# RWKV-5 attention and squared-ReLU MLP on one core: a new loading head, v through GpSimd's queue, and a new order table

## The chip, the core and the metric

The kernel runs on one core of a Trainium2 chip. Time is device time in microseconds; of the kernel before there are three runs, with a median of 171.05 us (170.32 to 171.6). The profile shown is of one execution.

## The reference

Four sequences (B), eight heads (H), 768 tokens (S) and 48 numbers a head (D). For every batch and head a 48x48 state is carried over the tokens, and the 8x48 = 384 outputs of a token go through a two-layer MLP with 2048 hidden numbers:

```python
for t in range(S):
    kt, vt, rt = k[:, :, t], v[:, :, t], r[:, :, t]
    cur = np.einsum('bhd,bhe->bhde', u[None] * kt, vt)
    y[:, :, t] = np.einsum('bhd,bhde->bhe', rt, state + cur)
    state = w[None, :, :, None] * state + np.einsum('bhd,bhe->bhde', kt, vt)
x = y.transpose(0, 2, 1, 3).reshape(B * S, H * D)
h = x @ w_in
return np.maximum(h, 0.0) ** 2 @ w_out
```

Inputs and output are float32; the kernel multiplies in bfloat16 and adds in float32.

## The kernel before

The tokens are cut into six chunks of 128. A chunk of one sequence is a *unit*; unit i is chunk i // 4 of sequence i % 4, so there are 24. A unit's attention goes through these steps, each a function and a word of the order table:

- `rt`, `kt`, `vt`: its r, k and v are loaded, 192 KB each, 128 tokens on the partitions. `scale` (VectorE) multiplies r and k by powers of w that depend on the token, into `rkw`.
- r and k are turned so that head numbers lie on the partitions (`rkT`). For units 0 to 5, the head of the program, TensorE does it (`turn`, x = 0 for r and 1 for k) and ScalarE copies it out (`rkT`). From unit 6 on two units go together: one DMA transpose on SyncE's queue (`rkD`).
- `at` is the product of k and r for each head, `mask` (VectorE) keeps its upper triangle, `y` multiplies it by v and adds the state's share; `dv` and `yb` (VectorE) add the token's own term and write y in bfloat16. `d` or `s` give that term's sums, and `s` also the unit's own state, which `sadd`, `sdec` and `stb` add up for the next chunk.
- `y` is turned into `xT`, by TensorE for units 0 to 5 (`xturn`, `xT`) and by a DMA transpose for pairs (`xD`).

The MLP of a unit follows: `m1` is a quarter (a pair's eighth) of the first layer, `relu` (ScalarE) and `sqA` or `sqD` (square on ScalarE or VectorE) make g, `m2` is a quarter of the second layer, `osb` copies its sum out and `out` stores it. From unit 6 on `m1` works on two units at once. The weights come by GpSimd's queue with a cast, in quarters `I` and `O`.

In the head, r and k of units 0 to 5 are loaded so that a partition holds four tokens in a row of one pair of heads; a load is then two transfers of 96 KB, one for the even heads and one for the odd, with runs of four tokens (768 bytes) in memory. k in that layout isn't in token order, which the state needs, so that after the first turn k is turned back (`kb`, four TensorE transposes, and `kbT`, a ScalarE copy). v of units 0 to 5 comes by GpSimd's queue in token order, 192 KB a transfer; r, k and v of the later units come by SyncE's queue in pairs of 384 KB, in token order, whose runs in memory are one token of one head (192 bytes).

What stands where is written out by hand: the program goes through the words of `ORDER`, `name.unit.part@bank`, and each issues its instructions. Every engine and every queue runs its own instructions in that order and waits for semaphores; nothing reorders them. `fill.n` is n products of a constant tile on TensorE with no use of the result. PSUM has eight banks, which the number behind `@` names; a bank is used again when its reader is done.

Of the kernel before, what the change touches and what calls it, by code (L numbers as in the profile page):

```python
# [16 lines left out]
kt.0.0 kt.0.1 rt.0.0 rt.1.0 I.0 rt.1.1 vt.0 ktA.1.0 lnat.0 fill.26 log@4567 kt.1.1 lnat.1 ids rt.2.0 w.1 upper w.0  # L17
fill.8 cols@1 rt.2.1 wk scale.0.0 kt.2.0 zeros scale.0.1 wr fill.8 turn.0.0@2 kt.2.1 copied uwb turn.0.1@5 rkT.0.0
rt.3.0 rkT.0.1 vt.1 rk.0 fill.10 at.0@63 scale.1.0 rt.3.1 I.3 kb.0@4 mask.0.0 d.0@2 turn.1.0@7 I.2 kbT.0 kt.3.0
mask.0.1 rkT.1.0 vt.2 scale.1.1 vb.0 I.1 kt.3.1 fill.19 turn.1.1@4 dv.0 y.0@3 rkT.1.1 rt.4.0 yb.0 vb.1 rk.1 fill.9  # L20
kb.1@4 kt.4.0 scale.2.0 at.1@31 xturn.0@6 rt.4.1 mask.1.1 d.1@5 turn.2.0@2 xT.0 rkT.2.0 scale.2.1 kt.4.1 fill.5
m1.0.0@7 kbT.1 mask.1.0 turn.2.1@2 relu.0.0 dv.1 rt.5.0 fill.2 y.1@1 rkT.2.1 m1.0.3@4 yb.1 end rt.5.1 s.1@5
scale.3.0 relu.0.3 wend xturn.1@7 rk.2 at.2@26 xT.1 kb.2@0 mask.2.1 sqA.0.0 kt.5.0 d.2@4 turn.3.0@3 vt.3 s.0@7
sadd.1 rkT.3.0 m1.0.2@1 kt.5.1 scale.3.1 kbT.2 O.0 m1.1.0@6 mask.2.0 vb.2 relu.0.2 vt.4 turn.3.1@3 dv.2 m1.1.3@5
rt.6 rkT.3.1 sadd.0 O.1 y.2@1 relu.1.0 kt.6 m1.1.2@0 yb.2 relu.1.3 vt.5 at.3@72 rk.3 relu.1.2 kb.3@4 mask.3.1
xturn.2@6 sqA.1.0 O.2 m1.0.1@5 scale.4.0 xT.2 s.2@0 O.3 sqD.0.3 d.3@2 relu.0.1 m1.1.1@1 vb.3 mask.3.0 turn.4.0@3
kbT.3 m1.2.0@6 scale.4.1 relu.1.1 dv.3 m1.2.1@4 rkT.4.0 sqD.1.3 sqA.0.2 y.3@7 m1.2.2@1 scale.5.0 relu.2.1 sqD.1.1
m1.2.3@2 relu.2.2 sqD.0.1 s.3@5 sqA.1.2 turn.4.1@4 m2.0.0@3 sadd.3 relu.2.3 sadd.2 m2.1.0@1 rkT.4.1 yb.3 relu.2.0
m2.1.1 rk.4 vb.4 scale.5.1 kb.4@7 stb.1 xturn.3@6 at.4@42 kbT.4 m2.0.1 mask.4.1 xT.3 stb.0 s.4@5 mask.4.0 turn.5.0@6
m1.3.0@2 sqD.2.1 rkT.5.0 y.4@0 dv.4 relu.3.0 turn.5.1@6 rt.8 sadd.4 m1.3.3@7 rkT.5.1 yb.4 m2.1.2 sqA.3.0 sqA.2.0  # L30
m2.0.2 kt.8 xturn.4@2 m2.0.3 xT.4 scale.6.0 kb.5@5 osb.0 m2.1.3 scale.7.0 relu.3.3 m1.3.1@2 vtS.6 kbT.5 vb.5
m1.4.0@6 scale.6.1 scale.7.1 at.5@75 relu.4.0 m2.2.0@0 mask.5.0 osb.1 rkD.6 sqA.4.0 m1.4.1@4 sqD.2.3 sqA.2.2 sqD.3.3
m1.4.2@1 relu.3.1 mask.5.1 m2.2.1 stb.3 sdec.4 m1.4.3@6 relu.4.2 rt.10 rk.5 y.5@5 sqA.4.2 scale.8.0 s.5@2 scale.8.1
relu.4.1 m2.2.2 scale.9.0 relu.4.3 vtS.8 m1.3.2@1 sqD.3.1 stb.4 m2.3.0@4 dv.5 relu.3.2 yb.5 m2.2.3 scale.9.1 kt.10
m2.3.1 osb.2 sadd.5 sqA.4.1 m2.4.0@1 sqD.4.3 vb.6 xturn.5@0 sdec.5 at.6@2376 xT.5 rk.6 rkD.8 m2.4.1 stb.2 mask.7.0
stb.5 m1.5.0@0 sqA.3.2 mask.6.0 s.7@7 relu.5.0 mask.7.1 m1.5.3@5 mask.6.1 s.6@2 relu.5.3 m2.4.2 dv.6 out.0 vb.8
y.6@3 dv.7 rt.12 y.7@0 yb.6 m1.5.1@6 yb.7 m2.3.2 sadd.6 relu.5.1 xD.6 scale.10.0 m2.4.3 sqA.5.0 scale.10.1 sqA.5.1
m2.3.3 sadd.7 vtS.10 osb.4 m1.5.2@6 scale.11.1 scale.11.0 m2.5.0@3 relu.5.2 sqD.5.3 kt.12 m2.5.1 sqA.5.2 rk.8
at.8@1520 osb.3 sdec.6 m2.5.2 mask.9.0 rkD.10 m2.5.3 mask.8.0 s.8@4 mask.8.1 osb.5 s.9@2 m1.6.0@7 mask.9.1 m1.6.1@6
sadd.8 relu.6.0 dv.9 kt.14 m1.6.3@5 relu.6.1 dv.8 m1.6.7@1 sqA.6.0 scale.12.0 sadd.9 sqA.6.1 y.9@3 rt.14 y.8@4 vb.10  # L40
m1.6.2@0 yb.8 stb.6 m1.6.5@2 yb.9 relu.6.3 sdec.9 xD.8 m1.6.4@6 relu.6.5 scale.12.1 m2.7.0@3 relu.6.2 sqD.6.3
relu.6.7 vtS.12 m2.6.0@4 scale.13.0 relu.6.4 scale.13.1 m1.6.6@7 sqA.6.2 rk.10 at.10@6120 sqA.6.4 rkD.12 m2.6.1
relu.6.6 mask.10.0 sqA.6.5 s.10@5 sdec.7 m2.7.1 sqA.6.6 sqD.6.7 m2.7.2 stb.7 mask.10.1 stb.9 out.1 m2.7.3 sadd.10
kt.16 mask.11.0 y.10@6 osb.7 m1.8.0@1 dv.10 m1.8.1@2 rt.16 scale.14.0 relu.8.0 sdec.8 m1.8.3@5 relu.8.1 mask.11.1
m2.6.2 stb.8 yb.10 sqA.8.1 s.11@3 y.11@2 relu.8.3 dv.11 m1.8.6@1 vb.12 yb.11 m1.8.4@6 relu.8.6 sadd.11 xD.10 m2.6.3
rk.12 sqA.8.0 relu.8.4 scale.15.0 m1.8.2@2 scale.14.1 m1.8.5@0 relu.8.2 sdec.10 out.4 m2.9.0@7 osb.6 scale.15.1
vtS.14 sqA.8.2 sqD.8.3 m2.8.0@6 relu.8.5 out.3 at.12@4312 sqA.8.6 rkD.14 s.12@0 sqA.8.5 mask.13.0 m2.8.1 sqA.8.4
mask.12.1 m1.8.7@5 mask.12.0 m1.10.1@1 relu.8.7 mask.13.1 out.2 m1.10.3@3 relu.10.1 scale.16.0 vtS.16 s.13@4 sadd.12
y.12@2 dv.12 rt.18 m2.8.2 sdec.11 m1.10.6@5 yb.12 m1.10.5@0 dv.13 relu.10.6 sqD.8.7 y.13@2 stb.10 m2.9.1 relu.10.5
scale.17.0 yb.13 sqA.10.6 m2.8.3 sadd.13 relu.10.3 xD.12 m1.10.2@0 osb.8 sqD.10.3 sqA.10.1 m1.10.0@3 scale.16.1  # L50
kt.18 m1.10.7@1 relu.10.0 scale.17.1 rt.20 at.14@5642 relu.10.2 rk.14 sqA.10.0 m2.9.2 mask.15.1 vb.14 m2.9.3
mask.14.0 rkD.16 relu.10.7 m1.10.4@2 mask.14.1 sqA.10.2 mask.15.0 s.15@5 stb.11 s.14@0 sqA.10.5 m2.11.0@3 dv.14
osb.9 y.14@4 relu.10.4 y.15@6 kt.20 yb.14 vb.16 m2.11.1 sdec.12 sqA.10.4 m2.10.0@1 sadd.15 stb.12 out.5 dv.15
m1.12.0@2 sqD.10.7 m1.12.1@7 relu.12.0 yb.15 m1.12.3@4 scale.18.0 xD.14 scale.18.1 m2.10.1 relu.12.3 scale.19.0
m1.12.7@6 relu.12.1 rt.22 m2.10.2 relu.12.7 out.7 m1.12.2@7 sqA.12.0 vtS.18 sqD.12.7 m2.11.2 sdec.13 relu.12.2
# [28 lines left out]
def kernel(  # L84
# [21 lines left out]
    NH = 6  # L106
# [516 lines left out]
```

## Time and profile before

| | |
|---|---|
| runs | 171.6, 170.32, 171.05 us; median 171.05 |
| profiled execution, first to last instruction (its span) | 170.2 us |
| TensorE busy | 163.9 us, 96% of the span |
| TensorE's weight loads | 134.1 us, 79% |
| ScalarE busy | 129.8 us, 76% |
| VectorE busy | 122.3 us, 72% |
| GpSimd busy | 15.7 us, 9% |
| mean granted TensorE clock | 0.988 |
| read from and written to HBM | 20.50 and 4.72 MB |

The span is what the profile measures between the first and the last instruction; a run's time has a little around it (the median is 0.85 us above this span). Busy time of TensorE counts matmuls whose ends are modelled, so that it says where TensorE had something in its queue rather than what it was worth. The chain of waits lists, in order of time, the pieces of work that the end depended on: start, length, engine and line. In the timeline a row gives start, length, engine, line, operation, output and inputs, and how often, with the idle time before it and what ended it in brackets; `SPq` and `POOLq` are the queues of SyncE and GpSimd, where the length is that of issuing.

### The profile page before, as it was taken

What the parts mean: (1) busy time and instruction counts of PE and PEld (TensorE: products, weight loads), DVE (VectorE), ACT (ScalarE), POOL (GpSimd) and SP (SyncE); (2) the same over time, 40 slices, a digit from 0 to 9 for tenths busy, and PEclk for the clock granted to TensorE, in tenths of its full rate; (3) what the DMA queues carried; (4) which work ended last, traced back from release to release, by engine and by line L of the source; (5) the groups of instructions that cost most, each with busy time, mean ns of one, the idle gap of its engine ahead of it and who ended that gap; (6) DMA issues with size and microseconds to landing.
All of it is one profiled execution on the core that took longest, in us unless ns stands there. A gap on an engine that the chain in (4) does not pass through costs nothing.

```text
span 170.2 us, 4733 instructions
## 1 busy us (share of the span) xinstructions
PE 163.9 (96%) x1947; PEld 134.1 (79%) x1947; DVE 122.3 (72%) x243; ACT 129.8 (76%) x255; POOL 15.7 (9%) x36
## 2 busy tenths in 40 slices
PE   7959999999999999999999999999999999999993
PEld 7649999778787697886977887787889789688672
DVE  6567999876999989988988888989697662101100
ACT  3735999888796489698499679688699739599921
POOL 7770670000000000000000000000000000000000
PEclk9996999999999999999999999999999999999999
DMA  3999999999999899999999997998990501100044
GB/s 92 172 279 240 272 194 254 213 201 227 185 181 218 153 214 190 181 212 191 236 182 202 174 251 173 188 288 197 180 232 4 179 6 54 42 0 4 0 164 162
DMA packets 91493, 28.86 MB, mean 170 GB/s; under 512 B 82864, under 2 KB 90672, under 8 KB 91472
## 3 DMA queue, kind: packets, MB, share of 16 engines
q1 hardware_dynamic: 88416, 23.99, 67.5%
q0 software_dynamic: 2624, 4.33, 12.9%
q8 instruction: 15, 0.25, 0.6%
q10 hardware_dynamic: 432, 0.25, 0.6%
q14 instruction: 6, 0.05, 0.1%
HBM read 20.50 MB, written 4.72 MB: 148 GB/s over the span
## 4 chain that ended last, share of the span: by engine, by line
PE 87%; DMA 6%; DVE 3%; SPq 2%; issue 1%; DVEq 0%
PE bank L493 36%; PE bank L517 34%; DMA rt<-in_r_dram 4%; PE bank L369 4%; PE bank L441 3%; DMA xT<-yb 2%; PE bank L398 2%; PE bank L447 2%; SPq L281 2%; PE bank L533 2%; PE bank L333 1%; PE bank L410 1%; PE bank L345 1%; PE bank L216 1%; PE bank L477 1%
## 5 line engine op out<-in xcount | busy, mean ns | idle before, releaser
L493 PE MATMUL bank<-xT,w_in_q 128*128 128x256 bf16 (+1 forms) x720 | 72.6, 251 | 0.1
L501 ACT ACTIVATE gr<-bank 128x512 f32<-128x512 f32 x96 | 55.3, 604 | 19.0 <-PE bank L493 15.2
L517 PE MATMUL bank<-w_out_q,g 128*128 128x384 bf16 x368 | 68.6, 326 | 0.0
L493 PEld LDWEIGHTS <-w_in_q 128*128 128x128 bf16 x720 | 63.8, 113 | 3.9 <-DMA xT<-yb 0.3
L517 PEld LDWEIGHTS <-g 128*128 128x128 bf16 x368 | 34.3, 98 | 18.1 <-issue 0.2
L508 ACT ACTIVATE g<-gr 128x512 bf16<-128x512 f32 x68 | 41.2, 636 | 0.2
L377 DVE TENSOR_TENSOR am<-bank,smask 128x512 bf16<-128x512 f32 x48 | 31.3, 684 | 7.4 <-PE bank L369 6.6
L510 DVE TENSOR_TENSOR g<-gr 128x512 bf16<-128x512 f32 x28 | 19.0, 686 | 17.2 <-ACT gr L501 17.2
L524 ACT COPY osb<-bank 128x384 f32<-128x384 f32 x23 | 11.0, 480 | 5.7 <-PE bank L517 5.6
L456 DVE TENSOR_TENSOR yb<-bank,dv 128x384 bf16<-128x384 f32 x24 | 12.9, 553 | 3.2 <-PE bank L447 2.3
L420 DVE TENSOR_TENSOR dv<-vb,bank 128x384 f32<-128x384 bf16 x24 | 13.0, 548 | 2.2 <-PE bank L410 1.4
L432 ACT CAST stb<-st 128x384 bf16<-128x384 f32 x20 | 10.2, 522 | 0.6 <-DVE st L428 0.6
L301 DVE TENSOR_TENSOR rkw<-rt,wpos 128x384 bf16<-128x384 f32 x18 | 9.8, 551 | 0.8 <-DMA rt<-in_r_dram 0.7
L301 DVE TENSOR_TENSOR rkw<-kt,wneg 128x384 bf16<-128x384 f32 x18 | 9.7, 551 | 0.8 <-DMA kt<-in_k_dram 0.8
L337 ACT COPY rkT<-bank 128x512 bf16<-128x512 bf16 x12 | 7.0, 590 | 3.4 <-PE bank L333 3.4
L216 PE MATMUL bank<-warm 128*128 128x128 bf16 x87 | 8.4, 265 | 1.1 <-DVE warm L161 1.1
L441 PE MATMUL bank<-vb,am 128*128 128x48 bf16 x192 | 8.9, 185 | 0.0
L428 DVE TENSOR_TENSOR st<-st,wend 128x384 f32<-128x384 f32 x16 | 8.8, 550 | 0.0
L424 DVE TENSOR_TENSOR st<-bank,st 128x384 f32<-128x384 f32 x16 | 8.7, 549 | 0.0
L441 PEld LDWEIGHTS <-am 128*128 128x128 bf16 x192 | 7.9, 97 | 0.8
L369 PE MATMUL bank<-rkT 64*128 64x128 bf16 x192 | 8.2, 221 | 0.2 <-ACT rkT L337 0.2
L216 PEld LDWEIGHTS <-warm 128*128 128x128 bf16 x87 | 7.0, 121 | 1.2 <-DVE warm L161 1.0
(75 smaller groups left out, 120.8 us busy)
## 6 DMA issues: line engine op xcount, KB each, us to landing
out_dram<-osb SPq DMA_DIRECT2D x23, 192.0 KB, 2.4
rt<-in_r_dram SPq DMA_DIRECT2D x9, 384.0 KB, 5.8
kt<-in_k_dram SPq DMA_DIRECT2D x9, 384.0 KB, 5.2
vt<-in_v_dram SPq DMA_DIRECT2D x9, 384.0 KB, 4.5
w_in_q<-in_moe_w_in_dram POOLq DMA_DIRECT2D x4, 384.0 KB, 8.3
w_out_q<-in_moe_w_out_dram POOLq DMA_DIRECT2D x4, 384.0 KB, 8.8
vt<-in_v_dram POOLq DMA_DIRECT2D x6, 192.0 KB, 7.3
kt<-in_k_dram SPq DMA_DIRECT2D x11, 96.0 KB, 5.2
```

Of the source, the lines that this page charges most:

```text
L216: nc.tensor.matmul(out=banks[0][:, :128], lhsT=warm, rhs=warm, start=True, stop=True)
L301: nc.vector.tensor_tensor(t["rkw"][:, x, :, :, :D], pair(src), pair(wneg if x else wpos), ALU.mult)
L369: nc.tensor.matmul(out=t["at"][o][:, p, :], lhsT=t["rkT"][sl, 1, p, :], rhs=t["rkT"][sl, 0, p, :], start=True, stop=True,)
L377: nc.vector.tensor_tensor(am, t["at"][o], smask.unsqueeze(1).to_broadcast([C, HP, C]), ALU.mult)
L420: nc.vector.tensor_tensor(t["dv"], t["vb"], t["d"].unsqueeze(2).to_broadcast([C, H, D]), ALU.mult)
L441: nc.tensor.matmul(out=y[:, 2 * p + o, :], lhsT=t[f"am{o}"][:, p, :], rhs=t["vb"][:, 2 * p + o, :], start=(o == 0 and p == 0), stop=c == 0 ...
L456: nc.vector.tensor_tensor(t["yb"], t["y"], t["dv"].rearrange("p h d -> p (h d)"), ALU.add)
L493: nc.tensor.matmul(out=t["h", s][:, a], lhsT=turned, rhs=chunks[c]["xT"][:, b : b + m, n, :], start=(n == 0), stop=(n == NK - 1),)
L501: nc.scalar.activation(t["gr", s], t["h", s], AF.Relu)
L508: nc.scalar.activation(g, x, AF.Square)
L510: nc.vector.tensor_tensor(g, x, x, ALU.mult)
L517: nc.tensor.matmul(out=t["o"], lhsT=chunks[units[i][0]]["g"][:, f, units[i][1], :], rhs=w_out_q[f // 4][:, f % 4, :], start=(f == 0), stop ...
```

## The change

1. **Head.** r of units 0 to 5 and k of units 0 and 1 keep the layout of four tokens a partition, but come as one transfer of 192 KB. k of units 2 to 5 is loaded in token order by GpSimd's queue, scaled with the token powers `wneg` that the later units use, and turned once; `kb` and `kbT` are left for units 0 and 1 alone. The first transfers are k of unit 0 on ScalarE's queue and r of units 0 and 1 on SyncE's.
2. **Constants.** The identity matrices and the triangle come from one iota on GpSimd and three VectorE comparisons, not from GpSimd's helpers; the ones and zeros under the columns of w and u are set by VectorE.
3. **v.** v of units 6 to 23 comes by GpSimd's queue, one transfer of 192 KB a unit, not by SyncE's in pairs.
4. **Order.** The whole table is new. `fill` products go from 87 to 42, with 34 of them at the very beginning; squares on ScalarE from 68 to 64 and on VectorE from 28 to 32; banks and the order of quarters of `m1` and `m2` differ (`m2` may begin with any quarter).

```diff
 ORDER = """
-kt.0.0 kt.0.1 rt.0.0 rt.1.0 I.0 rt.1.1 vt.0 ktA.1.0 lnat.0 fill.26 log@4567 kt.1.1 lnat.1 ids rt.2.0 w.1 upper w.0
...
+ktA.0 tab rt.1 wu.0 wu.1 upper ids vt.0 I.0 vt.1 lnw lnat.0 fill.33@1 fill.1@0 w.0 log@4567 lnat.1 scale.0.0 w.1
...
-    first = two("rt", 0, loads, [C, H, D], F32)[:, 0]
-    halves = lambda src: src.rearrange("(a o) (q l) d -> o q a (l d)", o=2, l=4)
-    nc.scalar.dma_start(out=first[:, 4:].rearrange("p l d -> p (l d)"), in_=halves(r[0, :, :C])[1])
+    of_two("rt", 0, loads, [C, H, D], F32)
+    by_four = lambda src: src.rearrange("(a o) (q l) d -> q a o (l d)", o=2, l=4)
+    nc.sync.dma_start(out=tiles[0]["rt"].rearrange("p (o l) d -> p o (l d)", o=2), in_=by_four(r[0, :, :C]))
...
+    apart_i = const.tile([128, 128], I32)
+    nc.gpsimd.iota(apart_i, pattern=[[1, 128]], base=0, channel_multiplier=-1)
...
     def identities():
-        make_identity(nc, ident4)
-        make_identity(nc, identb)
+        nc.vector.tensor_scalar(identb, apart_i, 0.0, None, ALU.is_equal)
+        nc.vector.tensor_scalar(ident4, apart_i[:HP, :HP], 0.0, None, ALU.is_equal)
 
     def upper():
-        make_upper_triangular(nc, smask, val=1.0, diag=False)
+        nc.vector.tensor_scalar(smask, apart_i, 0.0, None, ALU.is_gt)
...
+    def turned(i):
+        return i < NH and f" kb.{i}@" in ORDER.replace("\n", " ")
...
+        if i >= NH and not alone:
+            nc.sync.dma_start(out=whole.rearrange("s b h d -> s (b h) d"), in_=both(src, i))
+        elif i < NH and (name == "rt" or turned(i)):
             (queue or nc.sync).dma_start(
-                out=tiles[i][name][:, o * 4 : o * 4 + 4].rearrange("p l d -> p (l d)"), in_=halves(src)[o]
+                out=tiles[i][name].rearrange("p (o l) d -> p o (l d)", o=2), in_=by_four(src[b, :, c * C : (c + 1) * C, :])
             )
+        else:
+            nc.gpsimd.dma_start(out=tiles[i][name], in_=src[b, :, c * C : (c + 1) * C, :].rearrange("h s d -> s h d"))
...
-        if i >= NH:
+        if i >= NH or x and not turned(i):
             nc.vector.tensor_tensor(t["rkw"][:, x, :, :, :D], pair(src), pair(wneg if x else wpos), ALU.mult)
...
-    def load_v(i):
+    def load_v(i, whole_pair=False):
         c, b = units[i]
         whole = of_two("vt", i, loads, [C, H, D], F32)
-        if i >= NH:
+        if whole_pair:
             nc.sync.dma_start(out=whole.rearrange("s b h d -> s (b h) d"), in_=both(v, i))
         else:
             nc.gpsimd.dma_start(out=tiles[i]["vt"], in_=v[b, :, c * C : (c + 1) * C, :].rearrange("h s d -> s h d"))
```

Three places show what the new table does.

**VectorE in the head** (`rkw0` belongs to units 0 and 1, `rkw1` to units 2 and 3; `rt_88` and `kt_155` or `kt_153` are r and k of units 0 and 1, `am` the masked product, `rk` the product r times k). Before:

```order
L303 TENSOR_TENSOR rkw0_127<-rt_88,wfour_123 128x8x48
L303 TENSOR_TENSOR rkw0_127<-kt_155,wfour_123 128x8x48
L253 COPY cols_126<-bank1_77 128x8
L360 TENSOR_TENSOR rk_267<-rkT_241 128x512
L303 TENSOR_TENSOR rkw0_127<-rt_88,wfour_123 128x8x48
L377 TENSOR_TENSOR am0_294<-bank6_257,smask_135 128x512
L377 TENSOR_TENSOR am1_307<-bank3_79,smask_135 128x512
L303 TENSOR_TENSOR rkw0_127<-kt_155,wfour_123 128x8x48
```

Now:

```order
L219 TENSOR_SCALAR smask_133<-apart_i_94 128x128
L215 TENSOR_SCALAR identb_100<-apart_i_94 128x128
L216 TENSOR_SCALAR ident4_99<-apart_i_94 4x4
L242 TENSOR_TENSOR lnat_120<-lnw_119,at4_110 128x384
L244 TENSOR_TENSOR lnat_120<-lnat_120,lnw_119 128x384
L313 TENSOR_TENSOR rkw0_125<-rt_88,wfour_121 128x8x48
L313 TENSOR_TENSOR rkw0_125<-kt_153,wfour_121 128x8x48
L258 COPY cols_124<-bank0_76 128x8
L313 TENSOR_TENSOR rkw0_125<-rt_88,wfour_121 128x8x48
L313 TENSOR_TENSOR rkw0_125<-kt_153,wfour_121 128x8x48
L372 TENSOR_TENSOR rk_271<-rkT_230 128x512
L389 TENSOR_TENSOR am1_277<-bank2_78,smask_133 128x512
```

Three comparisons stand ahead of the powers, and both scalings of unit 1 now stand ahead of the first mask and not around it.

**GpSimd's queue in the head** (`w_in_q0` and so on are the weight quarters, `uwb` is made of u's columns and `d` needs it). Before:

```order
L168 DMA wu_95<-in_w_dram 4x2x48
L169 DMA wu_95<-in_u_dram 4x2x48
L288 DMA w_in_q0_147<-in_moe_w_in_dram 128x3x512
L311 DMA vt_162<-in_v_dram 128x8x48
masks.py:197 MEMSET ident4_100 4x4
```

Now:

```order
L222 DMA wu_96<-in_u_dram 4x2x48
L321 DMA vt_162<-in_v_dram 128x8x48
L298 DMA w_in_q0_145<-in_moe_w_in_dram 128x3x512
L321 DMA vt_162<-in_v_dram 128x8x48
L231 MEMSET uwb_134 128x32
L232 MEMSET wend_144 128x384
L293 DMA kt_226<-in_k_dram 128x8x48
L298 DMA w_in_q3_148<-in_moe_w_in_dram 128x3x512
L293 DMA kt_226<-in_k_dram 128x8x48
L261 TENSOR_TENSOR cols_124<-cols_124 128x4
```

v of units 0 and 1 now goes ahead of and right behind the first weight quarter, k of units 2 and 3 (`kt_226`) stands around the second, and `uwb` behind all of them.

**SyncE's queue around xT of units 10 and 11.** Before:

```order
L309 DMA vt_1429<-in_v_dram 128x16x48
L322 DMA_TRANSPOSE rkT_1465<-rkw2_129 128x16x128
L553 DMA out_0_dram<-osb_939 128x384
L278 DMA kt_1505<-in_k_dram 128x16x48
L278 DMA rt_1538<-in_r_dram 128x16x48
L467 DMA_TRANSPOSE xT_1409<-yb_1559 128x6x128
```

Now:

```order
L332 DMA_TRANSPOSE rkT_1401<-rkw2_127 128x16x128
L287 DMA rt_1404<-in_r_dram 128x16x48
L565 DMA out_0_dram<-osb_887 128x384
L565 DMA out_0_dram<-osb_1040 128x384
L479 DMA_TRANSPOSE xT_1363<-yb_1490 128x6x128
```

Between the turn of r and k of units 12 and 13 and xT there is one load now and were two, and the load of v ahead of them is gone from this queue.

More of the change, by code (lines that the diff above doesn't have):

```diff
@@ L22 @@
[L22 to L31, printed above, removed]
@@ L586 @@
             for _ in range(int(a[0])):
-                fill()
+                fill(where)
             continue
```

173 lines of the change are left out of this document (91 added, 82 removed).

## The prediction

> **What bounds the kernel now.** The page first: who is busy, and what each DMA queue moved.
>
> ```profile
> span 170.2 us, 4733 instructions
> PE 163.9 (96%) x1947; PEld 134.1 (79%) x1947; DVE 122.3 (72%) x243; ACT 129.8 (76%) x255; POOL 15.7 (9%) x36
> q1 hardware_dynamic: 88416, 23.99, 67.5%
> q0 software_dynamic: 2624, 4.33, 12.9%
> ```
>
> TensorE looks full, but a fill counts as busy too. So next the chain of waits, in order of time (start, length, what):
>
> ```profile
> 3.67 6.36 DMA rt<-in_r_dram
> ...
> 16.37 0.72 PE bank L493 x12
> ...
> 23.74 0.67 PE bank L493 x12
> ...
> 36.99 0.22 PE bank L345 x4
> ...
> 56.85 0.55 PE bank L369 x16
> ...
> 59.35 2.62 PE bank L493 x24
> ...
> 76.81 3.79 DMA xT<-yb
> 80.65 1.50 PE bank L493 x12
> ...
> 104.03 0.66 PE bank L493 x6
> 104.69 0.65 PE bank L517 x4
> ...
> 167.36 0.29 DVE osb L545
> ```
>
> The first layer's products (L493) begin at 16.4 us, and behind them the chain is TensorE almost without a break to 167.3. Adding the groups by such rows (a quarter of `m1` 0.67 us for one unit, an eighth 0.66 for a pair, a quarter of `m2` 0.65, the small steps by their own rows) I get 149.4 us of work from the first `m1` to the last `m2`, in 151.0 us. So there are two places for a gain: the start of `m1`, and the work. What the start waits for, in the timeline of VectorE:
>
> ```profile
> 5.83 0.60 DVE L303 TENSOR_TENSOR rkw<-rt,wfour 128x384 bf16<-128x384 f32 x1 [1.00 <-ACT wfour L242]
> 10.13 0.56 DVE L303 TENSOR_TENSOR rkw<-rt,wfour 128x384 bf16<-128x384 f32 x1 [1.63 <-DMA rt<-in_r_dram]
> 10.60 1.28 DVE L377 TENSOR_TENSOR am<-bank,smask 128x512 bf16<-128x512 f32 x2
> ```
>
> Unit 1's r is on the way until 10.0 us, and unit 0's two masks stand behind it on VectorE though their product was there earlier. The third bound is DMA. The same 384 KB from SyncE's queue take 14.7 us to land when they are issued among the weights, 4.5 in the middle of the run (issues in the stretch 20 to 21.3 us, then of the whole run):
>
> ```profile
> rt<-in_r_dram SPq DMA_DIRECT2D x1, 384.0 KB, 14.7
> ...
> vt<-in_v_dram SPq DMA_DIRECT2D x9, 384.0 KB, 4.5
> w_out_q<-in_moe_w_out_dram POOLq DMA_DIRECT2D x4, 384.0 KB, 8.8
> vt<-in_v_dram POOLq DMA_DIRECT2D x6, 192.0 KB, 7.3
> rkT<-rkw SPq DMA_TRANSPOSE x9, 6.3
> xT<-yb SPq DMA_TRANSPOSE x9, 3.1
> ```
>
> and the windows (us; busy time of PE, PEld, DVE, ACT, POOL; granted clock; DMA share; GB/s) show the engines of DMA full through the middle, with nothing left over:
>
> ```profile
> 8.00:9.00 1.00, 0.81 (x16) 0.61 (x16) 0.43 (x1) 0.18 (x2) 1.00 (x2) 1.00 1.14 327
> 9.00:10.00 1.00, 0.00 (x0) 0.00 (x0) 0.00 (x0) 0.33 (x1) 1.00 (x2) 1.00 1.07 335
> 13.00:14.00 1.00, 1.00 (x18) 1.00 (x15) 0.63 (x2) 0.95 (x2) 0.00 (x0) 0.50 1.16 215
> 16.00:17.00 1.00, 1.00 (x21) 1.00 (x19) 1.00 (x3) 1.00 (x3) 0.00 (x0) 1.00 1.13 284
> 40.00:50.00 10.00, 10.00 (x142) 7.98 (x141) 9.97 (x20) 9.01 (x19) 0.00 (x0) 1.00 0.96 189
> ```
>
> **The change, part by part.** The sum is made against the profiled execution: 170.2 us, 0.85 below the median of the runs, which I add at the end.
>
> *Start of the first layer.* On VectorE the three comparisons and two memsets come ahead of the powers of w. The trace has none on a 128x128 integer; the nearest rows are a copy of 128x128 and the wait that they fill:
>
> ```profile
> 1.44 0.23 DVE L179 COPY ones<-here 128x128 f32<-128x128 f32 x1
> 3.67 0.56 DVE L237 TENSOR_TENSOR lnat<-lnw,at 128x384 f32<-128x384 f32 x1 [0.36 <-ACT lnw L190]
> 4.86 0.94 ACT L242 ACTIVATE wfour<-lnat 128x384 f32<-128x384 f32 x2 [1.22 <-DVE lnat L239]
> ```
>
> About 0.8 us more, 0.36 of it idle now: the powers start 0.45 late, at 4.1. But r's power no longer stands behind k's on ScalarE, and each power needs only its own half. So r of unit 0 is scaled at 5.2, k at 5.8. r of unit 1 is now the second transfer of its queue and not the fourth and fifth; k of unit 1 is the third. Issues of such loads took 0.6 to 0.8 us each, so they go out by 2.3 us rather than 5, ahead of weights and v, and I take both as there by 7.0. Then VectorE has the two scalings to 7.5, `rk` to 8.0 and the masks to 9.2, where the masks ended at 11.9 before. v of unit 0 is issued ahead of the weight quarter and stands in no one's way. `d` waits for `uwb`, which now stands behind six issues of 0.8 to 0.95 us on GpSimd and ends at 9.0: just in time for `dv` at 9.2. Unit 1's turns go out to 9.6 (13.6 before), its `at` is done by 10.3, `yb` of unit 0 at 10.7, `xT` at 11.6. What the first `m1` now also stands behind are both turns of unit 2, whose k comes by GpSimd: issued at 5.8 behind 0.4 MB of v and one weight quarter. At the rate of the rows above it lands near 11 and is scaled by 12.8. I put the first `m1` at 13.3, 3.1 us earlier. Ends: if k of unit 2 takes the 9.1 us that the slowest v on that queue took here (an answer of the DMA view, 192.0 KB below), the gain is 0.5; if nothing waits, 3.6.
>
> ```profile
> vt<-in_v_dram POOLq DMA_DIRECT2D x1, 192.0 KB, 9.1
> ```
>
> *Work on TensorE.* `kb` of units 2 to 5 goes: four times 0.22 us, 0.9. Two turns are done ahead of the first `m1` that stood behind it, 0.44, and two fills, 0.1. The work from the first `m1` on is 147.9 us: 1.4 less. ScalarE loses four copies and four squares, VectorE gains four squares of 0.69 us; both have idle time in the middle and are costed at nothing. If that cover were gone, four squares are 2.7 us.
>
> *Clock.* From 9 to 10.7 us TensorE did nothing, and from 12.3 to 15.6 its clock was at half (window 13 to 14: 0.50). It was 1.00 again from 16 on, when `m1` began. The new head has 42 fills for 87, and none between 5 and 11 us. So I expect half clock when `m1` starts, for about 2.4 us of which half is lost: 1.2. Ends 0 (the window falls well) and 2.5.
>
> The Trainium skill says in "TensorE: Matmul & The Clock Gate", Part 1, that the clock halves after an idle window of about 3.4 us and comes back after a busy one of the same length; the trace agrees (3.3 us at half). By that rule alone the loss would be at most 1.7 us.
>
> *Waits for DMA.* Up to the turns of units 8 and 9 the kernel before needed 56.9 us (its `at`, L369 x16), with DMA full from 6 us on. What must have moved by then hardly changes: the same r, k, v and weights. The work for TensorE up to that `at` is 44.5 us by the groups and the `m1` start gives 53.2 with the clock. DMA brings its input perhaps 2 us earlier than before, because one load of v less stands ahead of each turn on SyncE's queue and v's rows travel in fewer packets (six loads of 1024 rows of 192 bytes and all weights made 2624 packets on GpSimd's queue). So `at` of 8 waits about 1.0 (0 to 3.6, all that was gained).
>
> Later, the distance from a pair's last `y` to its first `m1` is shorter. For units 10 and 11 there stood five eighths of `m1`, four quarters of `m2`, an `at` and small steps, 6.7 us; now three, two and the `at`, 3.8. What the way took:
>
> ```profile
> 74.21 0.56 DVE L456 TENSOR_TENSOR yb<-bank,dv 128x384 bf16<-128x384 f32 x1
> ...
> 73.78 2.93 SPq L278 DMA_DIRECT2D rt<-in_r_dram  x1
> 76.81 2.05 SPq L467 DMA_TRANSPOSE xT<-yb  x1
> ```
>
> `yb` ended at 74.8, xT went out only at 76.8 because a load's issue held the queue, and landed at 80.6. Without the load it is 0.7 and 3.1 to 3.8: 3.8 to 4.5, against 3.8. I take 0.5 (0 to 1.6). The other pairs have 4.6 us or more and cost nothing in the middle case.
>
> *Sum:* -3.1 - 1.4 + 1.2 + 1.0 + 0.5 = -1.8. The tail behind the last `m2` is the same. 170.2 - 1.8 = 168.4 for a profile, 169.2 for the median.
>
> **The rivals.** *The queues keep up.* No half clock and no new waits: -4.5, 166.5 us. For it: DMA on SyncE's queue gets nine loads of 4.5 us less. Against: DMA share 0.96 to 1.16 in every window shown.
>
> *The engines of DMA set the pace.* Both queues feed the same engines; if these are full, the turns of units 8 and 9 come when they came, at 56.9, the head's gain waits there, and from that `at` on the work is 109.6 us against 109.5: 171.1, no change. The Trainium skill states the rule in "DMA: Bandwidth & Descriptors", "Issuing engines are not separate DMA queues": issuing from several engines saves only issue time. The trace has the collision (14.7 against 4.5 us), not the sum of v's two ways.
>
> *Slower: transposes late at every pair.* The new table leaves 6.0 and 6.2 us of TensorE work between the last scaling and `at` for units 10 and 16, where the least was 8.4, and 3.8 to 5.2 from `y` to `m1` for four pairs, where it was 6.7. With the median landing (6.3, plus 0.55 for the scaling) the two `at` lose 0.9 and 0.7; with landings as slow as the longest ones here (7.7 for rkT, 4.7 for xT) all places together lose 7.4. Halfway is 4.4; with -2.3 from head, work, clock and units 8 and 9 that is +2.1, 173.2 us. It decides once the places together lose more than 2.3. For it: v's transfers on GpSimd's queue now fall between the transposes. Against: nine loads fewer ahead of them.
>
> ```profile
> DMA to landing us min/median/max: 4.4/6.3/7.7
> ...
> DMA to landing us min/median/max: 2.5/3.1/4.7
> ```
>
> **How the numbers follow.** Forecast 0.46, with its own range 167.8 to 170.6; queues keep up 0.19; DMA sets the pace 0.18; slower 0.17, since four pairs and three `at` have less room at once and one late landing makes the next `yb` late too. A measurement tells about 1% from no change, which is 169.3 to 172.8 here. The forecast lies on both sides of 169.3, a little over half below: faster 0.25 + 0.19 = 0.44, same 0.21 + 0.18 = 0.39, slower 0.17. The range of 8 in 10 takes in most of the first and the third rival and half of the last: 166.4 to 173.2.
>
> **What would show it.** In the profile after: the first `m1` at 12.8 to 14.5 us in the chain; half clock in the window of 13 to 15; TensorE's first longer pause behind the head ahead of `at` of units 8 or 10 with rkT as its releaser, or ahead of `m1` of 10 with xT; VectorE's longest wait on r's DMA gone; rows of L345 down to 8. It is wrong if `m1` starts at 15 or later (k of unit 2 late), if no DMA row stands behind 30 us in the chain and the time is near 166.5, or if several transposes do and it is over 171.

## The result and the profile after

The changed kernel takes 188.36 us (median of 4 runs, 185.88 to 189.72) against 170.69 us before. The ratio is 1.097 (95% interval 1.089 to 1.106): 17.7 us slower, where 169.2 was forecast and 173.2 was the end of the range. (Some executions are disturbed and slower whatever the kernel: ratios leave them out, and below the profiles of the kernel without most of v, of the six moved words, of the other sequence of loads and of the old head with the new rest are of such ones.) The page of the profile, its span, TensorE and the two DMA queues (packets, MB, share of 16 engines' time):

```profile
span 186.8 us, 4602 instructions
PE 167.6 (90%) x1886; PEld 134.5 (72%) x1886; DVE 126.0 (67%) x252; ACT 126.7 (68%) x247; POOL 33.8 (18%) x51
q1 hardware_dynamic: 68576, 19.67, 54.3%
q0 software_dynamic: 4032, 8.66, 22.1%
```

TensorE was busy for 96% of the span and is at 90%. The chain of waits names the reason: where it was TensorE's own products from 16 us on, it now goes through DMA six times; five of these (start, length, what):

```profile
7.12 31.79 DMA rt<-in_r_dram
...
51.52 10.18 DMA rkT<-rkw
...
72.79 4.80 DMA xT<-yb
...
83.02 4.41 DMA xT<-yb
...
89.37 12.69 DMA rkT<-rkw
```

r of units 6 and 7 took 31.8 us to land: issued at 7.12 for 20.34 before, it was there at 38.9 for 35.0. Their `at` still began on time (47.30 for 47.61), so that the loss lies behind it. The transposes `rkT` of units 8 and 9 and of 14 and 15 took 10.2 and 12.7, where 7.7 was the longest before. TensorE's waits for these (total, times, longest), and two windows with the granted clock behind the two long ones (0.70 and 0.66; all of the middle ran at 1.00 before):

```profile
PE bank L381 <- DMA rkT<-rkw: 10.8, 3, 5.8
PE bank L502 <- DMA xT<-yb: 1.9, 2, 1.5
```

```profile
60.00:70.00 10.00, 8.26 (x84) 6.38 (x85) 6.59 (x13) 3.29 (x7) 0.00 (x0) 0.70 1.08 213
100.00:110.00 10.00, 7.89 (x78) 5.93 (x79) 5.00 (x9) 4.05 (x9) 0.00 (x0) 0.66 0.78 168
```

Here a long pause costs twice: the wait, and then products at a lower clock. From the first `m1` on, TensorE stood still for 12.7 us in the timeline. The first `m1` came 1.6 us earlier (14.66 against 16.26), some 1.4 us of work are gone, and the span is 16.6 longer: 6.9 us are left for slower products, a remainder and not a measured term.

What made the transposes late stands in the timelines of GpSimd's and SyncE's queues:

```profile
41.53 2.63 POOL L321 DMA_DIRECT2D vt<-in_v_dram  x3 [12.64 <-ACT vb L328]
47.27 2.63 POOL L321 DMA_DIRECT2D vt<-in_v_dram  x3 [3.11 <-ACT vb L326]
...
82.75 2.63 POOL L321 DMA_DIRECT2D vt<-in_v_dram  x3 [8.95 <-ACT vb L326]
91.36 1.76 POOL L321 DMA_DIRECT2D vt<-in_v_dram  x2 [5.97 <-ACT vb L326]
```

```profile
7.12 30.29 SPq L287 DMA_DIRECT2D rt<-in_r_dram  x2
...
51.52 6.52 SPq L332 DMA_TRANSPOSE rkT<-rkw  x1
...
84.91 4.35 SPq L287 DMA_DIRECT2D rt<-in_r_dram  x1
89.37 5.19 SPq L332 DMA_TRANSPOSE rkT<-rkw  x1
```

GpSimd has little to do and issues v as soon as a buffer of an older pair is free, three units in a burst, just ahead of the two slow transposes; these also took 6.5 and 5.2 us to issue, where 4.4 was the longest before. In the kernel before, v stood in SyncE's queue behind what was due before it.

### The profile page after: what moved, and what is told of

It reads as the page before. It is cut to its first block, busy times and chain, and to the rows that moved or that the text cites. A ratio compares the mean times of both kernels' runs of the same rounds, so it can differ in the third digit from the quotient of the medians.

```text
span 186.8 us, 4602 instructions
## 1 busy us (share of the span) xinstructions
PE 167.6 (90%) x1886; PEld 134.5 (72%) x1886; DVE 126.0 (67%) x252; ACT 126.7 (68%) x247; POOL 33.8 (18%) x51
## 4 chain that ended last, share of the span: by engine, by line
PE 54%; DMA 38%; SPq 3%; DVE 3%; ACT 1%; issue 0%; DVEq 0%
PE bank L502 24%; PE bank L529 21%; DMA rt<-in_r_dram 17%; DMA rkT<-rkw 16%; DMA xT<-yb 5%; PE bank L381 3%; SPq L289 2%; PE bank L453 1%; PE bank L545 1%; PE bank L459 1%; PE bank L410 1%; DVE yb L468 1%; PE bank L422 1%; SPq L287 1%; DVE g L521 1%; DVE rkw L311 1%
## 5 line engine op out<-in xcount | busy, mean ns | idle before, releaser
L502 PE MATMUL bank<-xT,w_in_q 128*128 128x256 bf16 (+1 forms) x720 | 75.6, 255 | 1.9 <-DMA xT<-yb 1.9
L529 PE MATMUL bank<-w_out_q,g 128*128 128x384 bf16 x368 | 69.7, 335 | 0.0
L529 PEld LDWEIGHTS <-g 128*128 128x128 bf16 x368 | 35.6, 100 | 20.4 <-issue 2.2
L519 ACT ACTIVATE g<-gr 128x512 bf16<-128x512 f32 x64 | 38.3, 628 | 0.3
L521 DVE TENSOR_TENSOR g<-gr 128x512 bf16<-128x512 f32 x32 | 21.5, 686 | 16.2 <-ACT gr L510 16.2
L321 POOL DMA_DIRECT2D vt<-in_v_dram x24 | 21.4, 894 | 54.7 <-ACT vb L326 39.3
L536 ACT COPY osb<-bank 128x384 f32<-128x384 f32 x23 | 10.8, 479 | 16.2 <-PE bank L529 16.2
L381 PE MATMUL bank<-rkT 64*128 64x128 bf16 x192 | 9.2, 240 | 11.0 <-DMA rkT<-rkw 10.8
L311 DVE TENSOR_TENSOR rkw<-kt,wneg 128x384 bf16<-128x384 f32 x22 | 11.8, 551 | 7.7 <-DMA kt<-in_k_dram 7.7
L381 PEld LDWEIGHTS <-rkT 64*128 64x128 bf16 x192 | 6.3, 104 | 14.5 <-DMA rkT<-rkw 12.6
L369 DVE TENSOR_TENSOR rk<-rkT 128x1024 bf16<-128x1024 bf16 x9 | 6.2, 686 | 8.5 <-DMA rkT<-rkw 8.5
```

The lines of the kernel that those rows point to most:

```text
L311: nc.vector.tensor_tensor(t["rkw"][:, x, :, :, :D], pair(src), pair(wneg if x else wpos), ALU.mult)
L321: nc.gpsimd.dma_start(out=tiles[i]["vt"], in_=v[b, :, c * C : (c + 1) * C, :].rearrange("h s d -> s h d"))
L381: nc.tensor.matmul(out=t["at"][o][:, p, :], lhsT=t["rkT"][sl, 1, p, :], rhs=t["rkT"][sl, 0, p, :], start=True, stop=True,)
L502: nc.tensor.matmul(out=t["h", s][:, a], lhsT=turned, rhs=chunks[c]["xT"][:, b : b + m, n, :], start=(n == 0), stop=(n == NK - 1),)
L519: nc.scalar.activation(g, x, AF.Square)
L521: nc.vector.tensor_tensor(g, x, x, ALU.mult)
```

## The experiments

Three theories: P (packets on a second queue), O (the new order leaves too little distance) and H (the new head). Line numbers in the rows are those of each kernel. The kernel before had 170.6 to 171.2 us as median beside these runs; ratios are to it, with 95% intervals.

### v back on SyncE's queue

```diff
-... vt.6 ... vt.7 ... vt.17 ... vt.23        # GpSimd, a unit each
+... vtS.6 rkD.6 ... vtS.8 rkD.8 ... vtS.22   # SyncE, a pair each
```

> The changed kernel, with v of units 6 to 23 again by SyncE's queue in pairs of 384 KB, each ahead of or near the transpose that it stood by before; head, constants, fills and the rest of the new table stay. Theory P (packets): while GpSimd's queue has work, each DMA engine gives a packet to the one queue and a packet to the other in turn, so that the 192-byte packets of SyncE's queue crawl beside packets of 1 to 4 KB; v on GpSimd's queue is what costs. It expects 168 to 174 us, r of units 6 and 7 landed by 33 us instead of 38.9, and no wait of TensorE over 2 us behind the head. Rival O (order): the new table leaves too little work between the scaling and at, whoever brings v: 183 to 188. Rival H (head): k of units 2 to 5 on GpSimd's queue and the half clock are what costs: 176 to 182, with r of units 6 and 7 still at 36 or later.

The casts of v of units 16, 20 and 22 move with it. 176.51 us, ratio 1.028 (1.019 to 1.038): 11.9 of the 17.7 us are back. That is above P's range and at the lower end of H's. TensorE's waits in its profile (span 173.0):

```profile
PE bank L500 <- DMA xT<-yb: 2.2, 2, 2.0
...
PE bank L527 <- DVE dv L430: 1.0, 1, 1.0
PE bank L420 <- DVE dv L430: 0.9, 1, 0.9
...
PE bank L379 <- DMA rkT<-rkw: 0.4, 1, 0.4
```

The waits for `rkT` are gone (0.4 for 10.8); two of `dv` and one of `xT` are left. Yet r of units 6 and 7 still landed at 36.4 us, not by 33, as H had it: the starving among the weights is not v's doing alone. Two thirds of the loss come with v on the second queue, then, and one third is open.

### The kernel before with v on GpSimd's queue

```diff
-            nc.sync.dma_start(out=whole..., in_=both(v, i))
+            for j in (i, i + 1):
+                nc.gpsimd.dma_start(out=tiles[j]["vt"], ...)
```

> The kernel before with one edit: v of units 6 to 23 by GpSimd's queue, 192 KB a unit, at the places in the table where the pairs stood. P: slower by 6 to 16 us (177 to 187), with rkT landing over 9 us at some pairs (7.7 at most before). O and H: 170 to 172, as before, or a little faster, since SyncE's queue has nine loads fewer.

176.77 us, ratio 1.032 (1.024 to 1.040): 6.1 us slower by this edit alone, at the lower end of what P expected, and against O and H. But not at the place that P named: `rkT` landed in 5.4 us as median and 8.7 at most. The largest wait is VectorE's, 6 us in front of the scaling of r:

```profile
40.46 1.03 DVE L299 TENSOR_TENSOR rkw<-rt,wpos 128x384 bf16<-128x384 f32 x2 [5.95 <-DMA rt<-in_r_dram]
```

`at` of units 6 and 7 began at 52.4 for 47.6. So loads suffer as well as transposes.

### The changed kernel without most of v

```diff
-... vt.8 ... vt.23
-            nc.scalar.copy(whole, two("vt", i, ...))
+            nc.scalar.copy(whole, twos["vt", 3])
```

> The changed kernel without v's transfers of units 8 to 23; the casts read the v of units 6 and 7 again, so only 3.1 MB of DMA are left out. P: 168 to 171, all long waits for rkT gone. O: 183 or more, the waits stay where they are. H: about 178, the waits up to 62 us stay, those later go.

170.15 us, ratio 0.994 (0.990 to 0.999), and no wait of TensorE for a DMA behind the head. P holds so far: the whole loss needs v's traffic. But 166 to 167 would be its time if the head's gain arrived, so that P is not all.

### Fewer v at a time, and which v costs

```diff
-        whole = of_two("vt", i, loads, [C, H, D], F32)
+        whole = of_two("vt", i, loads, [C, H, D], F32, bufs=2)
```

> The changed kernel with two buffers for v's pairs instead of four and v's loads in the order of the units: no v of unit 6 on is issued before a pair two earlier has been cast, so that GpSimd's queue has fewer of v's bytes ahead of r of units 6 and 7, and no more than two units' v at once later. P: 174 to 182, since each v still goes beside a transpose or a load, but the bursts are gone. If only the bursts and the early prefetch are the matter: 168 to 173. O: 183 to 188.

179.30 us, ratio 1.047 (1.037 to 1.058). P's range: half of the loss stays with v in small portions; the longest DMA pieces of its chain behind the head are 8.9 (r), 7.7 and 9.2 us (`rkT`).

Then the changed kernel with v of units 6 to 9 alone by SyncE, and with v of units 10 to 23 alone by it:

```diff
-... vt.8 ... vt.6 ... vt.7 ... vt.9
+... vtS.6 rkD.6 ... vtS.8 rkD.8
```

> The changed kernel, with v of units 6 to 9 alone on SyncE's queue; 10 to 23 stay on GpSimd's. P: half of the 12 us comes back, the part at the weights: r of units 6 and 7 lands 2 us earlier, the wait for rkT of 8 and 9 (5.8 us, and half clock behind it) goes, those for rkT and xT behind 70 us stay: 180 to 184. If only what is issued early matters: 175 to 178. If only what is issued late matters: 187 to 189.

```diff
-... vt.10 ... vt.23
+... vtS.10 ... vtS.22
```

> The other half: v of units 6 to 9 by GpSimd's queue as in the changed kernel, 10 to 23 by SyncE's in pairs. P: 180 to 184, a wait for rkT of 8 and 9 at 55 to 62 us, none over 2 us later. If only the early issues matter: 186 to 188. If only the late ones: 175 to 178.

182.33 us (1.065; 1.057 to 1.073) and 176.16 (1.029; 1.023 to 1.036). My halves were wrong: early v on GpSimd's queue costs nothing when the later ones are on SyncE's (176.2 against 176.5 with none there), and the later ones cost 6 us without the early ones and 12 with them. What costs is v that is issued while transposes and loads are due; the early ones make that worse but don't begin it.

### Is it the second queue, or the size of the packets?

```diff
-vtS.6 ... vtS.22
+vtA.6 ... vtA.22    # nc.scalar.dma_start, a pair each
```

> As the run with v on SyncE's queue, but v's pairs are issued on ScalarE's queue: a second ring beside SyncE's, with packets of 192 bytes like those of SyncE's, not of 4 KB. P, with the size of the packets as what hurts: 174 to 180, no rkT over 9 us. If any second queue beside SyncE's hurts as much, since the DMA engines are full: 184 to 190, with rkT of 10 to 13 us. Nine issues on ScalarE cost it some 5 us, of which it has idle time enough.

177.71 us, ratio 1.038 (1.033 to 1.043): only 1.2 us above v on SyncE's queue. TensorE's waits for transposes add up to 6.3 us for 2.6 there, and the longest `rkT` took 10.2 us, so that my "no rkT over 9" failed; the time is in the range of the size. A second queue with small packets hurts much less than GpSimd's here. That the size is the reason isn't shown by this alone: on ScalarE's queue v is also issued at other times, where ScalarE's own work lets it. How the two queues share an engine shows where GpSimd's always has work: packets, MB and share in the changed kernel's window 25 to 30 us:

```profile
q0 software_dynamic: 366, 1.01, 95.7%
q1 hardware_dynamic: 366, 0.07, 11.9%
```

One packet for one packet, but 2.8 KB for 0.2 KB (573 and 569 in the window 20 to 25). Most of GpSimd's packets there are the weights': with v on SyncE's queue the counts from 25 to 30 are 350 and 354. With v on SyncE's queue GpSimd's begins to run dry in the window 30 to 35, and SyncE's moves 0.54 MB there; in the changed kernel, where v follows the weights, it is 0.10:

```profile
q1 hardware_dynamic: 2823, 0.54, 56.8%
q0 software_dynamic: 209, 0.57, 48.3%
```

```profile
q0 software_dynamic: 379, 1.12, 92.9%
q1 hardware_dynamic: 516, 0.10, 14.7%
```

At the two slow transposes it is another picture (changed kernel, windows 52 to 56 and 95 to 102 us):

```profile
q1 hardware_dynamic: 2132, 0.41, 68.7%
q0 software_dynamic: 122, 0.36, 42.8%
```

```profile
q1 hardware_dynamic: 1698, 0.59, 74.6%
q0 software_dynamic: 117, 0.35, 38.8%
```

The counts are far from one for one. The trace shows two other things there. v's packets of 4224 bytes took 0.31 us each in the first window and 0.65 in the second, for 0.24 from 30 to 35. And of the 16 signals that tell of the landing of k issued at 44.45, fifteen came by 53.2 and the last at 56.3, while the transpose behind it was being issued until 58.0. Whether taking turns, longer packets or one late part that holds SyncE's queue makes these transposes late is therefore open; that v's queue does is what the runs show.

### v behind the transposes

```diff
+    def gate(i):
+        nc.gpsimd.tensor_copy(seen, tiles[i + 1]["rkT"][:, 1, 3, :1])
-... vt.10 ... vt.23
+at.8 gate.8 vt.10 vt.11 vt.12 vt.13 ... at.18 gate.18 vt.22 vt.23
```

> The changed kernel, v of units 6 to 9 as there; from unit 10 on GpSimd reads one element of the rkT of a pair just landed before it issues the v of a later pair, so that v goes by the same queue but begins only when the transpose has landed. If v's packets hurt the transposes that they run beside: rkT back under 9 us and 176 to 181. If they hurt the loads of r and k as much, which then are what v runs beside: 183 to 188.

189.46 us, ratio 1.107 (1.099 to 1.114). v no longer starts beside the transpose that it is gated on, and the loss stays. But it meets the next one: an `rkT` issued at 72.71, between two loads of v let go at 72.60 and 73.47, took 11.7 us, so that "rkT back under 9 us" failed. VectorE also waits for k, whose load went out together with four v that had just been let go:

```profile
57.27 3.51 POOL L321 DMA_DIRECT2D vt<-in_v_dram  x4
```

```profile
68.13 0.56 DVE L311 TENSOR_TENSOR rkw<-kt,wneg 128x384 bf16<-128x384 f32 x1 [5.56 <-DMA kt<-in_k_dram]
```

So v hurts what is due beside it, loads and transposes, and a gate that lets v go in bursts is no cure. Which of the two loses more, this run doesn't tell.

### The rest: head or order?

I first tried to mend the three waits that were left with v on SyncE's queue:

```diff
-rt.14 kt.12 ... vtS.16 ... out.2 ... xD.12 ... vtS.22 rkD.20 ... rk.20 ... dv.18
+kt.12 rt.14 vtS.10 ... xD.12 out.2 vtS.16 ... rkD.20 vtS.22 ... dv.18 rk.20
```

> The run with v back on SyncE's queue (176.5 us, 173.0 in its profile) and six words moved: the load of k of units 12 and 13 ahead of r of 14 and 15 and of v of 10 and 11; v of 16 and 17 and a store behind the transpose xT of 12 and 13; v of 22 and 23 behind the transpose rkT of 20 and 21; rk of 20 and 21 behind dv of 18. They go at the three longest waits left there: 0.98 us for dv, 1.97 for xT, 0.92 for dv. If the rest of the loss is the new table's short distances, as O has it for this part: 171 to 174. If the rest is the head with k of units 2 to 5 on GpSimd's queue (H): 175 to 178, no change.

179.07 us, ratio 1.038 (1.032 to 1.044): no gain. The transposes were not late (`rkT` 7.0 us at most, `xT` 3.1), but TensorE waited for ScalarE instead. Behind v's later load the likely cause is a cast of v that holds ScalarE; I have not shown that.

```profile
PE bank L457 <- ACT stb L442: 3.1, 1, 3.1
```

At one place both tables have issued the same work to TensorE: behind `m2.4.0` here and `m1.5.2` there, just ahead of `at` of units 8 and 9. There they can be joined both ways, with v on SyncE's queue:

```diff
-ORDER = """<new head> m2.4.0 <new rest>"""
+ORDER = """<new head> m2.4.0 <rest of the table before>"""
```

> Two tables joined where both have issued the very same work to TensorE (behind the fourth quarter of m2 of unit 4, at the products at of units 8 and 9): the new head up to there, v of units 6 to 23 on SyncE's queue, and from there on the words of the table before. If the head is worth its 2.0 us (at of 6 and 7 started at 45.6 in the run with v on SyncE's queue, at 47.6 before) and the rest of the loss lies in the new table behind that place (O, for this part): 168 to 170 us, faster than before. If the loss comes from the head (H): 173 to 177.

```diff
-ORDER = """<old head> m1.5.2 <old rest>"""
+ORDER = """<old head> m1.5.2 <rest of the new table>"""
```

> The opposite join: the head of the kernel before up to the same place, and from there on the words of the new table, v on SyncE's queue. O: 174 to 178, with waits for xT, kT or dv of 1 to 2 us behind 60 us. H: 170 to 171.5, as before.

New head and old rest: 174.24 us, ratio 1.016 (1.010 to 1.022). Old head and new rest: 175.66 to 179.95 in four executions, the lowest 4.8 us above before. So the new rest costs about 2 us behind the new head (176.51 to 174.24) and about 5, by that lowest one alone, behind the old one (O); but the head, which I expected to gain, loses 3.4 in front of the old rest. At `at` of 8 and 9 it was 2.4 us ahead (54.37 for 56.78), then TensorE waited where it never waits before, and at `at` of 12 and 13 nothing was left (78.49 for 78.29):

```profile
PE bank L500 <- DMA xT<-yb: 2.3, 2, 1.2
PE bank L379 <- DMA rkT<-rkw: 1.3, 1, 1.3
```

Is that the sequence of SyncE's loads, which the joined table takes from both?

```diff
-rkD.6 rt.12 kt.10 rt.10 vtS.8 rkD.8 xD.6 vtS.10 rt.14 kt.12 rkD.10 kt.14
+rkD.6 rt.10 vtS.8 kt.10 rkD.8 rt.12 xD.6 vtS.10 kt.12 rkD.10 kt.14 rt.14
```

> The joined kernel with the new head (174.2 us), with SyncE's queue from the transpose of units 6 and 7 on in the sequence of the kernel before: r of units 10 and 11 directly behind that transpose, r of 12 and 13 and of 14 and 15 each one transpose later, and the scaling of unit 13's r behind that of unit 12. If the head's 2.4 us are lost because loads that are not yet needed stand ahead of rkT and xT: at of 10 and 11 starts by 64.5 instead of 65.6 and 169 to 171.5 us. If DMA cannot bring the input of units 8 to 13 earlier, in whatever sequence: 173 to 175.

174.37 us, ratio 1.017 (1.012 to 1.022). No: another sequence, the same time. Then both without v of units 8 to 23:

```diff
-... vtS.8 ... vtS.22
-            nc.scalar.copy(whole, two("vt", i, ...))
+            nc.scalar.copy(whole, twos["vt", 3])
```

> The joined kernel with the new head without v's transfers of units 8 to 23 (the casts read v of 6 and 7 again). If what takes the head's gain is the pace of DMA: 166.5 to 169, no wait of TensorE for rkT or xT. If it is the order of the words itself: 172 or more.

> The kernel before without v's transfers of units 8 to 23, to read the last run by. TensorE waits for no DMA there, so both theories expect 170 to 171, as with v.

170.31 us (0.995; 0.992 to 0.998) and 170.83 (0.998; 0.995 to 1.001). Without v no transpose is waited for, and the loss goes: the transfers together set the pace. The new head is 0.9 us ahead at `at` of 8 and 9 (56.00 for 56.91) and stays 0.9 ahead at 12 and 13. But even then it is worth 0.5 us by the medians, not 2 to 4, which neither theory had. Its profile shows half clock from 7.5 to 17.5 us. So I filled the pauses, in the new head and in the old:

```diff
+fill.10@1 cols@0 fill.2@1 turn.0.0@3 fill.3@2 turn.0.1@1 ... fill.6@4 at.0@32 ... fill.8@0 xturn.0@0 ...
```

> The joined kernel with the new head and 41 more fills in eight of TensorE's pauses before the first m1 (5 to 14 us), so that its clock does not fall to half. If the half clock is part of what keeps the head's gain from the end (it covered 7.5 to 17.5 us in the run without v, 3 us of that behind the start of m1): 1 to 1.5 us less than the joined kernel, 172.5 to 173.5. If the later waits for rkT and xT give it all back: 174 as before.

```diff
+... d.0@2 fill.28 turn.1.0@7 ...
```

> The kernel before with 28 more fills ahead of the first turn of unit 1, where TensorE idles 1.8 us, so that the half clock from 12.3 to 15.6 us goes. If the half clock holds up the first m1: it starts 0.5 to 1 us earlier and 170 to 170.5 us, faster than before. If m1 waits for loads: 171, no change.

172.24 us (1.005; 1.002 to 1.009) and 171.18 (1.001; 0.997 to 1.004). The new head gains 2.0 us by the fills, more than expected, but half clock doesn't explain it. Window 13 to 14 us of the joined kernel without the fills and with them has the same granted clock (1.00):

```profile
13.00:14.00 1.00, 0.57 (x10) 0.49 (x11) 0.71 (x2) 1.00 (x4) 1.00 (x2) 1.00 1.26 232
```

```profile
13.00:14.00 1.00, 0.93 (x17) 0.93 (x17) 1.00 (x4) 0.15 (x2) 1.00 (x2) 1.00 1.18 211
```

In the profile without them the clock was at half from about 8 to 11 us, and back before the first `m1` at 14.14. With them `m1` began later, at 14.95, and `at` of 8 and 9 at 55.95 for 54.37. And without them three executions with a mean granted clock of 0.99 took 172.70 to 173.90 us, two with 1.000 took 175.19 and 175.46. What shrank is the wait for transposes: 3.6 us without the fills, and with them only

```profile
PE bank L380 <- DMA rkT<-rkw: 1.1, 1, 1.1
```

So a head that comes 0.8 us later waits less behind it; why the fills do this I have not tested.

In the kernel before, fills moved the first `m1` in the profile from 16.26 to 14.78 us and the median by nothing: beside them, 17 of the 22 executions without the new fills show a mean granted clock of 1.000 anyway (spans 168.4 to 170.6).

At last, the one part of the head that looked free of risk, alone in the kernel before:

```diff
-kt.0.0 kt.0.1 rt.0.0 rt.1.0 I.0 rt.1.1 ...
+kt.0.0 rt.0.0 rt.1.0 I.0 ...           # a load is one DMA of [q a o (l d)]
```

> The kernel before with one part of the new head alone: r and k of units 0 to 5 come as one transfer of 192 KB in the same layout (r of unit 0 stays in halves), 11 issues fewer on the queues. r of unit 1 should land by 8.5 instead of 10.0 us and the first m1 start at 14.5 to 15.5 instead of 16.3. If that reaches the end: 169 to 170. If the weights' packets set when the loads land, whatever their number: 170.5 to 171.5.

172.64 us, ratio 1.009 (1.005 to 1.012): slower, outside both ranges. `at` of unit 1 came 1.5 us earlier (13.11 for 14.65), but the first `m1` at 16.25, now behind ScalarE's copy of `xT`, and the first weight quarter was late for the next:

```profile
16.25 0.83 PE L494 MATMUL bank<-xT,w_in_q 128*128 128x128 bf16 x12 [1.82 <-ACT xT L482]
17.91 0.86 PE L494 MATMUL bank<-xT,w_in_q 128*128 128x128 bf16 x12 [0.29 <-DMA w_in_q<-in_moe_w_in_dram]
```

No version here beats the kernel before.

## Why the prediction was wrong

The step that failed is the first sentence on DMA: "DMA brings its input perhaps 2 us earlier than before, because one load of v less stands ahead of each turn on SyncE's queue and v's rows travel in fewer packets". The two reasons are facts, one load less and fewer packets, but neither brought the input earlier. The 56.9 us that I took for the time DMA needed was `at` in TensorE's own order: in the kernel before the transpose of units 8 and 9 went out at 47.99 us and landed 5.1 us later, at 53.1.

```profile
47.99 3.60 SPq L322 DMA_TRANSPOSE rkT<-rkw  x1
...
rkT<-rkw SPq DMA_TRANSPOSE x1, 5.1
```

In the changed kernel it landed at 61.7 (51.52 + 10.18): not 2 us earlier but 8.6 later. With v on SyncE's queue in the same new table it was 54.5.

*Fewer packets are not less time.* Rows of the pages: the kernel before with v by GpSimd, then the new table with v by SyncE (the rows of the kernel before open the prediction, the changed kernel's open the result).

```profile
span 176.8 us, 4754 instructions
q1 hardware_dynamic: 69840, 20.45, 56.1%
q0 software_dynamic: 3776, 7.87, 21.1%
```

```profile
span 173.0 us, 4582 instructions
q1 hardware_dynamic: 87152, 23.21, 63.5%
q0 software_dynamic: 2880, 5.12, 13.6%
```

Share by span gives the time that the packets took, over 16 engines; packets overlap, since shares go above 1, so that it is a rough measure. In the kernel before SyncE's queue lost 114.9 - 99.2 = 15.7 us by v's move, and GpSimd's gained 37.3 - 22.0 = 15.3: nothing saved. In the new table it is 8.5 lost for 17.8 gained.

*One load less ahead is no gain when the load then runs beside.* In one queue v stood behind what was due before it. On a second queue it ran beside loads and transposes that were due now: among the weights one packet for one packet, with more bytes a turn, and later in a way that is open (see above). I had the row for it (14.7 against 4.5 us for the same load, beside weights and not) and took it for a matter of the weights only. The Trainium skill states this taking of turns in "DMA: Bandwidth & Descriptors", "Queues, rings and completion order": each engine goes round-robin between the queues that have work, packet by packet. The counts 366 and 366 from 25 to 30 us agree; those from 52 to 56, 2132 and 122, show no such turns. I weighed another rule of that page, on issue time, and not this one.

By the steps of the sum:

- *First `m1`*: forecast 13.3, measured 14.66. The order of events was right, also that k of unit 2 would be the last to come: its scaling came at 13.58, where I had the end at 12.8, and `m1` behind its turn. The gain was 1.6, not 3.1.

```profile
13.58 0.55 DVE L311 TENSOR_TENSOR rkw<-kt,wneg 128x384 bf16<-128x384 f32 x1
...
14.28 0.59 PE L341 MATMUL bank<-identb,rkw 128*128 128x128 bf16 x4
14.66 1.49 PE L502 MATMUL bank<-xT,w_in_q 128*128 128x128 bf16 x12
```

- *Work*: 1.4 us less; fits the runs without v. From the first `m1` to the end of the last product these take 151.4 (new head) and 150.9 us (before); with 0.5 us of pauses and some 1.3 of half clock (an estimate: half of the time at half clock behind `m1`) taken off the first, 1.3 us remain.
- *Clock*: forecast 1.2. It was at half until 18.4 us, 3.7 of them behind the first `m1`, so 1.9 if half of it is lost. Right in kind in this execution, and too short. The agreement with the rule cited there holds for the way back alone (3.3 us): ahead of the half clock TensorE was idle for 1.8 us, not 3.4.
- *Wait at `at` of 8 and 9*: forecast 1.0, end 3.6; measured 5.84 (start 61.74 for 56.78). The upper end was "all that was gained", since I let DMA at worst bring the transpose at 56.9. It fell 5 us behind that.
- *Wait for `xT`*: forecast 0.5 at units 10 and 11; 1.47 there and 0.45 at 8 and 9. Mis-sized by 1.4 us, right in kind.
- *Not in the sum*: `at` of units 14 and 15, 4.68 us behind a 12.7 us transpose, and a lower clock after each long pause.

The rival that had the direction, late transposes, was given 0.17 and 173.2 us. Its price came from the longest landings before (7.7 and 4.7 us); these are the longest where SyncE's queue had no v beside it, and no bound once it has. For "DMA sets the pace" the head's lost gain is shown too: 2.4 us ahead at `at` of 8 and 9 and gone by 78 us with v, 0.9 ahead and kept without.

How the 17.7 us add up by the medians: 11.9 for v's queue in the new table; 2.3 for the new table's rest (176.51 to 174.24); 2.0 that the fills gave back in the new head, with shorter waits in the profile and not by half clock; and 1.1 to 1.6 that is left and open. Each is one difference of medians with about 1 us of uncertainty, and they act on each other: v's queue costs 6.1 in the kernel before.

## What to carry to other kernels

One queue is also an order: here a transfer that was due late did no harm behind the ones that were due first, and the same transfers on a second queue cost 6.1 us in one table and 11.9 in another. Before moving loads to a queue "with room", list what will be in flight beside them and price these with the worst row of a stretch where both queues have work, not with the middle of the run. A head that starts earlier is worth only what DMA can deliver earlier: 2.4 us ahead at 54 us became nothing by 78.

## What the runs showed of the hardware

The clock fell to half without a long pause. In the joined kernel without v, windows 5 to 8 us show TensorE busy for 0.53, 0.68 and 0.84, with no wait over 0.3 us there in the timeline, and the granted clock at 1.00, 1.00 and 0.75, then 0.50 until 17:

```profile
5.00:6.00 1.00, 0.53 (x4) 0.38 (x5) 0.96 (x3) 0.93 (x3) 1.00 (x4) 1.00 1.02 244
6.00:7.00 1.00, 0.68 (x8) 0.34 (x6) 1.00 (x4) 0.97 (x3) 1.00 (x2) 1.00 1.00 234
7.00:8.00 1.00, 0.84 (x12) 0.57 (x12) 0.86 (x2) 0.98 (x2) 1.00 (x2) 0.75 0.90 207
```

Which share of busy time keeps the clock up, no run here shows.

And moving v to GpSimd's queue, from packets of 192 bytes to packets of some 4 KB (3840 and 4224 bytes), saved the DMA engines no time by their packets' records: for the 18 units 15.3 us more on GpSimd's queue for 15.7 less on SyncE's in the kernel before, and 17.8 more for 8.5 less in the new table.
